# Sums of values over two halves of the keys, in 64x32 tiles, for two of eight groups of heads

## The chip, the cores and the metric

The kernel runs on one core of a Trainium2 chip. The metric is device time in microseconds (us), from the first to the last instruction of one execution with what lies around it; less is better. A core has five engines that run at once and wait for each other by semaphores: TensorE (PE: matmuls; PEld: its weight loads), VectorE (DVE), ScalarE (ACT), GpSimd (POOL) and SyncE (SP, which issues most DMAs). Matmuls write to PSUM, eight banks of 128 partitions x 512 fp32 values; ACT and DVE read them from there.

## What is computed

Two layers of self-attention, each followed by a dense block with squared ReLU, with the same weights both times. The sequence has 2048 rows of 640 values, 32 heads of 20 values each. Cut to what matters:

```
qkv = (x @ wqkv).reshape(B, S, 3, H, Dh).transpose(2, 0, 3, 1, 4)
q, k, v = qkv[0], qkv[1], qkv[2]
scores = einsum("bhqd,bhkd->bhqk", q, k) * (Dh ** -0.5)
p = softmax(scores, axis=-1)
o = einsum("bhqk,bhkd->bhqd", p, v)
A(x) = o.transpose(0, 2, 1, 3).reshape(B, S, D) @ wo
...
x = x + A(layernorm(x));  x = x + B(layernorm(x))
x = x + A(layernorm(x));  x = x + B(layernorm(x))
```

## The kernel before

Everything is written by hand in program order; nothing is scheduled by a planner. A layer has three stages: `qkv` (projections, and a part of the maxima), `attention`, and the output projection with the dense block.

The 32 heads are taken in 8 groups of 4 (g = 0 to 7), the queries in 4 blocks of 512. A block of a group (t = 4 g + query block, 32 in a layer) goes through 16 key tiles of 128 keys; one key tile of one block is called a step here, so a layer has 512 steps. For each step `attention` issues:

- four scores (`score`, L560), one for each head: 128 keys x 512 queries into one of PSUM banks 0 to 3. Operands are fp32r. Of the four heads, two lie in partitions 0 to 61 ("a" in the order, `par` 0) and two in 64 to 125 ("b", `par` 1), so a score takes a 64x128 tile of the array, half of its rows, and two scores of different halves can run side by side. ACT takes the exponential (L567) into an SBUF tile `e`, in fp32;
- sums of values (`pv`, L572; "V" in the order): for each of the four heads one fp32 matmul of the values (128 keys x 32, a column of ones among them, which gives the softmax's denominator) with the exponentials (128 keys x 512 queries). A matmul of 128 rows and 32 columns takes a 128x32 tile, and the four heads lie side by side in the columns. All 16 steps of a block accumulate in bank 7. Each fp32 matmul is issued as two;
- about three maxima (`smax`, L463 and L475; "m" for `par` 0, "n" for `par` 1): softmax needs the largest score of each query beforehand. TensorE computes 128 queries x 512 keys in a 64x128 tile into one of banks 4, 5 and 6, taken in turn (`sm_ring`), and DVE reduces it to one column of `mx`. These belong to blocks some steps ahead; when a block's maxima are complete, they are turned into two more rows of the operand `q`.

The order within PE's program comes from written-out strings. `pairs()` chooses by how many maxima are still due how many of each kind (12 to 16) go into the next eight steps, and `ORDERS` has one string for each such number. At 12 it is:

```
12: "naambbmVanmbambVbmannabVnabnmabVabnmbanVbbmnanaVbmmbaanVbmbmnaaV",
```

Values of a step come one step after its scores: V of step i follows the scores of step i + 1. `state["begun"]` is the last step whose scores have begun, `state["done"]` the next one whose values are due. Within a half of the rows, or where a bank has to be free first, instructions wait in this order.

At the end of a block `finish` (L585) copies bank 7 to an SBUF tile `o` on DVE; POOL and DMAs then divide by the denominators. The whole PSUM is in use in this stage: banks 0 to 3 scores, 4 to 6 maxima, 7 values.

Of the kernel before, what the change touches and what calls it, by code (L numbers as in the profile page):

```python
# [16 lines left out]
P = 128  # L17
# [8 lines left out]
NQB = S // QB  # L26
NG = H // 4
NKT = S // P
# [11 lines left out]
def tile_layers(  # L40
# [11 lines left out]
    nc = tc.nc  # L52
# [10 lines left out]
    def name(p):  # L63
        n_alloc[0] += 1
        return f"{p}{n_alloc[0]}"

    def slot(shape, dtype, label):
        return arena.tile(shape, dtype, tag="slot", name=name(label))

    def dma(eng, dst, src):  # L70

        if dst.dtype == F32R:
            dst = dst.bitcast(F32)
        if src.dtype == F32R:
            src = src.bitcast(F32)
        eng.dma_start(dst, src)
# [4 lines left out]
    banks = psum.tile([P, 8, 512], F32, tag="banks", name="banks")  # L81
# [183 lines left out]
    def split_to(dst_hi, dst_lo, src):  # L265

        nc.scalar.copy(dst_hi, src)  # L267
        nc.vector.tensor_sub(dst_lo, src, dst_hi.bitcast(F32))  # L268
# [9 lines left out]
    def pool_hi(dst, src):  # L278
        nc.gpsimd.tensor_copy(dst, src)  # L279

    def pool_lo(dst, a, b):
        nc.gpsimd.tensor_sub(dst, a, b)  # L282
# [123 lines left out]
    k_t, q_t, v_t, mx_t, kept = {}, {}, {}, {}, {}  # L406
    left, done, split = {}, set(), {}
# [25 lines left out]
    def load_q(t):  # L433
        g, qb = divmod(t, NQB)
        q_t[t] = slot([P, 2, QB], F32R, "q")
        rows_of_heads(q_t[t], d_qk[0, :, :, qb * QB : (qb + 1) * QB], QSEG, g)
# [16 lines left out]
    def maxima(t):  # L453
        if t not in mx_t:
            mx_t[t] = small.tile([P, 4, 4, 4], F32, tag="mx", bufs=14, name=name("mx"))
            if t in PARTLY:
                nc.vector.memset(mx_t[t], LEAST)
        return mx_t[t]

    def by_queries(dst, t, p, sub, c, par):  # L460

        b = 64 * par
        nc.tensor.matmul(  # L463
            dst,
            q_t[t][b : b + 60, p, sub * P : (sub + 1) * P],
            k_t[t // NQB, c][b : b + 60, p, :],
            start=True,
            stop=True,
        )

    def smax(ring, t, p, sub, c, par):

        dst = ring("sm")
        by_queries(dst, t, p, sub, c, par)
        nc.vector.tensor_reduce(  # L475
            maxima(t)[:, 2 * p + par, sub, c : c + 1], dst, axis=AX.X, op=ALU.max
        )
# [73 lines left out]
    def score(t, kt, h, es):  # L551

        p, par = divmod(h, 2)
        if p not in es:
            es[p] = weights[len(e_n) % len(weights)]
            e_n.append(t)
        dst = ps_st("st")
        b = 64 * par
        assert t in done
        nc.tensor.matmul(  # L560
            dst,
            k_t[t // NQB, kt // 4][b : b + 62, p, (kt % 4) * P : (kt % 4 + 1) * P],
            q_t[t][b : b + 62, p, :],
            start=True,
            stop=True,
        )
        nc.scalar.activation(es[p][:, par, :], dst, AF.Exp, scale=SCALE)  # L567

    def pv(acc, t, kt, es, heads=(3, 2, 1, 0)):
        for h in heads:  # L570
            p, par = divmod(h, 2)
            nc.tensor.matmul(  # L572
                acc[32 * h : 32 * h + 32, :],
                v_t[t // NQB, kt // 8][:, kt % 8, 32 * h : 32 * h + 32],
                es[p][:, par, :],
                start=(kt == 0),
                stop=(kt == NKT - 1),
            )

    def finish(t, acc):  # L580


        g, qb = divmod(t, NQB)
        o = slot([P, 2, QB], F32, "o")
        nc.vector.tensor_copy(o[:, 0, :], acc)  # L585
        res = []

        def store(q):
            ot = res.pop().rearrange("p l t -> p (l t)")
            for h in range(4):  # L590
                r0 = (4 * g + h) * DH
                dma(q, d_o[r0 : r0 + DH, qb], ot[32 * h : 32 * h + DH])

        if t == NBLK - 1:

            def invert():
                dst = ps_all("rs")
                nc.tensor.matmul(dst, sums_t, o[:, 0, :], start=True, stop=True)
                nc.vector.reciprocal(o[:, 1, :], dst)

            def divide():
                nc.vector.tensor_mul(o[:, 0, :], o[:, 0, :], o[:, 1, :])
                res.append(slot([P, 2, QB], F32R, "ot"))
                split_to(res[0][:, 0, :], res[0][:, 1, :], o[:, 0, :])

            return [invert, divide, lambda: store(nc.scalar)]

        few = small.tile([P, 16], F32, tag="few", bufs=2, name=name("few"))
        for h in range(4):
            dma(nc.sync, d_s[t, h : h + 1], o[32 * h + DH : 32 * h + DH + 1, 0, :])  # L610

        def load():
            dma(nc.sync, few, d_s[t].rearrange("h (q j) -> (h q) j", j=16))

        def invert():
            nc.gpsimd.tensor_tensor(few, few, minus_t, op=ALU.pow)  # L616

        def spread():
            dma(nc.sync, d_r[t].rearrange("h (q j) -> (h q) j", j=16), few)

        def gather():
            for h in range(4):
                dma(nc.sync, o[32 * h : 32 * h + 32, 1, :], d_r[t, h].partition_broadcast(32))

        def divide():
            ot = slot([P, 2, QB], F32R, "ot")
            nc.gpsimd.tensor_mul(o[:, 0, :], o[:, 0, :], o[:, 1, :])  # L627
            pool_hi(ot[:, 0, :], o[:, 0, :])
            pool_lo(ot[:, 1, :], o[:, 0, :], ot[:, 0, :].bitcast(F32))
            res.append(ot)  # L630

        return [load, invert, spread, gather, divide, lambda: store(nc.sync)]
# [230 lines left out]
    def attention(first, x_src, first_rows):  # L863
# [3 lines left out]
        weights.extend(slot([P, 2, QB], F32, "e") for _ in range(6))  # L867
        st_n, sm_n = [0, 0], [0, 0]
        state = {"begun": -1, "done": 0, "acc": None, "debt": 0}
        sm_ring = Ring(4, 5, 6)  # L870
        todo = [
            (t, p, sub, c)
            for t in range(NBLK)
# [15 lines left out]
        rows = {"next": min(t for t in range(NBLK) if t not in done), "at": None}  # L889
# [33 lines left out]
        def op(o):  # L923
            if o in "ab":
                par = "ab".index(o)
                i, p = divmod(st_n[par], 2)
                if i >= last:
                    return
                st_n[par] += 1
                if i > state["begun"]:  # L930
                    state["begun"] = i
                    begin(i)
                score(i // NKT, i % NKT, 2 * p + par, es_of.setdefault(i, {}))
            elif o in "mn":
                par = "mn".index(o)
                n = sm_n[par]
                if n == len(todo):
                    return
                t, p, sub, c = todo[n]
                if n == firsts[t] and par == 0:  # L940
                    for s in blocks[blocks.index(t) :][:2]:
                        if s not in q_t:
                            load_q(s)
                if (t // NQB, c) not in k_t or t not in q_t:
                    return
                sm_n[par] += 1
                smax(sm_ring, t, p, sub, c, par)
                if n == ends[t] and min(sm_n) > n:
                    over.add(t)
                    if t * NKT > state["begun"] + 2 * NKT:  # L950
                        del q_t[t]
            else:
                i = state["done"]
                if i >= last or min(st_n) < 2 * (i + 1):
                    return
                t, u = divmod(i, NKT)
                if u == 0:
                    state["acc"] = banks[:, 7, :]
                pv(state["acc"], t, u, es_of.pop(i))
                state["done"] += 1  # L960
                if u == NKT - 1:
                    steps = finish(t, state["acc"])
                    split.update((i + j, f) for j, f in zip((4, 6, 7, 9, 11, 12), steps))
                t = rows["next"]
                if rows["at"] is not None:
                    if state["begun"] >= rows["at"]:
                        mrows_load(t)
                        rows.update(next=t + 1, at=None)
                elif t in over and t in q_t and state["begun"] >= (t - 2) * NKT + 4:
                    mrows_max(t)  # L970
                    mrows(t)
                    rows["at"] = state["begun"] + 2
# [13 lines left out]
        for o in "abab":  # L986
            op(o)
# [109 lines left out]
    def layer(first, x_a, x_m, x_e, front_0, ahead):  # L1097
        qkv(first, x_a, front_0)
        xs = []
        attention(first, x_a, xs)  # L1100
        steps = []
        for i in sorted(split):
# [120 lines left out]
```

## Time and profile before

| | us |
|---|---|
| median of the runs shown | 3796.79 |
| lowest and highest of the runs | 3794.22, 3799.36 |
| the profiled execution's own time | 3801.53 |
| its span, from the first to the last instruction | 3799.7 |
| PE busy in the span | 3705.0 (98%) |
| DVE busy | 2807.6 (74%) |
| ACT busy | 2556.0 (67%) |
| POOL busy | 831.0 (22%) |

The profile is of one execution. An instruction's row names the line of the kernel, the engine, the operation, the tiles that it writes and reads ("out<-in"), for matmuls rows*columns of the weights, the count, the time, and after a bar or in brackets how long the engine stood idle before it and what released it. Matmuls overlap, and their ends are modelled, so the start of the next one says more than the length of one. A timeline's rows give start and length in us from the span's start; instructions of one kind that follow closely are merged into one row with their count. The attention stages lie at about 366 to 1450 us and 2257 to 3342 us.

### The profile page before, as it was taken

The numbers are of one execution on the slowest core, as the hardware profiler recorded it, in microseconds if no ns is written. First come the engines' busy times: TensorE is split into PE (matmuls) and PEld (weight loads), VectorE is DVE, ScalarE is ACT, GpSimd is POOL, SyncE is SP. The second block draws the span as 40 slices with busy tenths as digits, with TensorE's granted clock in tenths as the row PEclk, the third lists the DMA queues.
The fourth block names the chain that finished last, engine by engine and source line by source line (L and its number), as shares of the span: only waits on it lengthen the run. The fifth ranks groups of instructions, "written<-read, shape, count | busy, mean of one in ns | idle before, by whom it ended". The sixth has DMA issues, their size and how long they took to land.

```text
span 3799.7 us, 64213 instructions
## 1 busy us (share of the span) xinstructions
PE 3705.0 (98%) x23572; PEld 2130.6 (56%) x23572; DVE 2807.6 (74%) x4796; ACT 2556.0 (67%) x4887; POOL 831.0 (22%) x921
## 2 busy tenths in 40 slices
PE   7999999999999999799999999999999999998999
PEld 5677343443444338688876764434444444387888
DVE  7788999999999973344467889999999999633443
ACT  2555999999999993112224459999999999921221
POOL 6530333321221110111154201122121211101110
PEclk9999999999999999899999999999999999998999
DMA  7564454432211136311255533222222111463111
GB/s 220 191 209 143 135 143 151 140 83 80 59 45 45 43 114 233 135 42 42 93 185 170 176 125 82 74 75 60 65 78 63 43 45 43 124 228 127 42 45 40
DMA packets 256530, 402.27 MB, mean 106 GB/s; under 512 B 67580, under 2 KB 114428, under 8 KB 256216
## 3 DMA queue, kind: packets, MB, share of 16 engines
q1 hardware_dynamic: 255672, 396.45, 33.6%
q8 instruction: 187, 3.06, 0.3%
q10 hardware_dynamic: 544, 1.71, 0.2%
q14 instruction: 127, 1.04, 0.1%
HBM read 261.22 MB, written 136.81 MB: 105 GB/s over the span
## 4 chain that ended last, share of the span: by engine, by line
PE 91%; DVE 4%; DMA 2%; ACT 1%; POOL 1%; issue 0%; SPq 0%; ACTq 0%; POOLq 0%; DVEq 0%
PE banks L572 27%; PE banks L560 20%; PE banks L297 18%; PE banks L463 15%; PE banks L308 6%; PE banks L355 4%; DVE h L268 1%; DVE mx L484 1%; DVE bst L255 1%; DMA w<-d_w 1%; DVE r L1070 1%; ACT h L267 1%; PE banks L385 0%; PE banks L1043 0%; DMA x<-d_x 0%
## 5 line engine op out<-in xcount | busy, mean ns | idle before, releaser
L567 ACT ACTIVATE e<-banks 128x512 f32<-128x512 f32 x4096 | 2114.4, 604 | 62.0 <-PE banks L560 3.5
L475 DVE TENSOR_REDUCE mx<-banks 128x1 f32<-128x512 f32 x2940 | 1847.1, 684 | 186.3 <-PE banks L463 114.0
L463 PE MATMUL banks<-k,q 60*128 60x512 f32 x3744 | 1156.0, 437 | 9.0 <-DMA q<-d_qk 7.3
L560 PE MATMUL banks<-q,k 62*128 62x512 f32 x4096 | 1152.2, 435 | 2.1 <-DVE mx L484 1.7
L572 PE MATMUL banks<-e,vg 128*32 128x512 f32 x8192 | 1092.1, 605 | 0.0
L560 PEld LDWEIGHTS banks<-q,k 62*128 62x128 f32 x4096 | 601.5, 185 | 697.4 <-ACT e L567 664.8
L463 PEld LDWEIGHTS banks<-k,q 60*128 60x128 f32 x3744 | 537.8, 185 | 335.6 <-DVE mx L475 206.3
L297 PE MATMUL banks<-w,h 128*128 128x320 f32 x2304 | 380.0, 323 | 51.6 <-ACT h L267 40.1
L297 PEld LDWEIGHTS banks<-w,h 128*128 128x128 f32 x2304 | 357.4, 197 | 66.1 <-ACT h L267 46.6
L572 PEld LDWEIGHTS banks<-e,vg 128*32 128x32 f32 x8192 | 161.7, 108 | 357.4 <-issue 330.3
L495 ACT ACTIVATE rl<-banks 128x512 f32<-128x512 f32 x352 | 191.3, 596 | 247.3 <-PE banks L463 247.1
L297 PE MATMUL banks<-xnT,w 128*128 128x512 f32 x1440 | 330.7, 390 | 0.0
L308 PE MATMUL banks<-xnT,wqk 128*128 128x512 f32 x1200 | 319.9, 410 | 1.3 <-POOL wqk L282 1.3
L1069 ACT ACTIVATE r<-banks,b_t 128x512 f32<-128x512 f32 x96 | 66.0, 688 | 370.8 <-PE banks L297 370.8
L505 DVE CUSTOM_DVE_ANT_0 rl<-banks,rl 128x512 f32<-128x512 f32 x352 | 229.2, 689 | 111.4 <-PE banks L463 101.6
L297 PEld LDWEIGHTS banks<-xnT,w 128*128 128x128 f32 x1440 | 270.2, 188 | 55.3
L484 DVE TENSOR_REDUCE mx<-banks 128x2 f32<-128x1024 f32 x226 | 271.7, 1220 | 20.0 <-PE banks L463 19.2
L308 PEld LDWEIGHTS banks<-xnT,wqk 128*128 128x128 f32 x1200 | 217.8, 191 | 85.9 <-issue 43.9
L616 POOL TENSOR_TENSOR few<-few,minus_t 128x16 f32<-128x16 f32 x62 | 179.8, 2900 | 285.7 <-DMA few<-d_s 285.7
L1089 DVE TENSOR_TENSOR x<-banks,x 128x320 f32<-128x320 f32 x128 | 62.8, 491 | 216.5 <-PE banks L297 216.5
L627 POOL TENSOR_TENSOR o<-o 128x512 f32<-128x512 f32 x62 | 79.6, 1283 | 620.5 <-DMA o<-d_r 342.4
L279 POOL CAST mr<-nt 128x32 fp32r<-128x32 f32 x64 | 13.4, 209 | 804.1 <-DVE nt L531 804.1
(73 smaller groups left out, 2019.7 us busy)
## 6 DMA issues: line engine op xcount, KB each, us to landing
q<-d_qk SPq DMA_DIRECT2D x744, 80.0 KB
d_qk<-ev SPq DMA_DIRECT2D x80, 512.0 KB
k<-d_qk SPq DMA_DIRECT2D x468, 80.0 KB
x<-d_x SPq DMA_DIRECT2D x88, 320.0 KB
d_o<-ot SPq DMA_DIRECT2D x248, 80.0 KB
ot<-d_o SPq DMA_DIRECT2D x38, 512.0 KB
d_v<-v SPq DMA_DIRECT2D x32, 512.0 KB
vg<-d_v SPq DMA_DIRECT2D x32, 512.0 KB
```

Source lines behind the costliest of these rows:

```text
L297: nc.tensor.matmul(dst, a, b, start=(n == 0), stop=(n == last))
L308: nc.tensor.matmul(dst, w_qk.piece(pos * 10 + hw * KD + k), xt_[tb][k][:, hx, :], start=(n == 0), stop=(n == 3 * KD - 1),)
L355: nc.tensor.matmul(dst[:, :HALF], xt_[tb][k][:, hx, i * P : (i + 1) * P], w_v.piece(k * 4 + hw * 2 + hf), start=(j == 0), stop=(j == 3 * K ...
L463: nc.tensor.matmul(dst, q_t[t][b : b + 60, p, sub * P : (sub + 1) * P], k_t[t // NQB, c][b : b + 60, p, :], start=True, stop=True,)
L475: nc.vector.tensor_reduce(maxima(t)[:, 2 * p + par, sub, c : c + 1], dst, axis=AX.X, op=ALU.max)
L484: nc.vector.tensor_reduce(maxima(t)[:, 2 * p : 2 * p + 2, sub, c], dst, axis=AX.X, op=ALU.max)
L495: nc.scalar.activation(res[par], dst[:, par, :], AF.Relu)
L505: nc.vector.tensor_tensor_reduce(out=r[par], in0=dst[:, par, :], in1=r[par], scale=1.0, scalar=LEAST, op0=ALU.add, op1=ALU.max, accum_out= ...
L560: nc.tensor.matmul(dst, k_t[t // NQB, kt // 4][b : b + 62, p, (kt % 4) * P : (kt % 4 + 1) * P], q_t[t][b : b + 62, p, :], start=True, stop ...
L567: nc.scalar.activation(es[p][:, par, :], dst, AF.Exp, scale=SCALE)
L572: nc.tensor.matmul(acc[32 * h : 32 * h + 32, :], v_t[t // NQB, kt // 8][:, kt % 8, 32 * h : 32 * h + 32], es[p][:, par, :], start=(kt == 0 ...
L616: nc.gpsimd.tensor_tensor(few, few, minus_t, op=ALU.pow)
```

## The change

In two of the eight groups of heads (numbers 4 and 6, counted from 0) the value sums are taken over two halves of a key tile: keys 0 to 63 go into bank 7, keys 64 to 127 into bank 6. Each matmul has 64 rows and 32 columns (a 64x32 tile), and there are eight of them in a step instead of four, each issued as two. At the end of such a block DVE copies the first bank and adds the second. While a step of such a group is begun or due, maxima take turns in banks 4 and 5 only. The order strings are as before, and so are all other groups.

```
+    HALVES = (4, 6)
+
     def pv(acc, t, kt, es, heads=(3, 2, 1, 0)):
+        n = P // len(acc)
         for h in heads:
             p, par = divmod(h, 2)
-            nc.tensor.matmul(
-                acc[32 * h : 32 * h + 32, :],
-                v_t[t // NQB, kt // 8][:, kt % 8, 32 * h : 32 * h + 32],
-                es[p][:, par, :],
-                start=(kt == 0),
-                stop=(kt == NKT - 1),
-            )
+            for i, a in enumerate(acc):
+                rows = slice(i * n, (i + 1) * n)
+                nc.tensor.matmul(
+                    a[32 * h : 32 * h + 32, :],
+                    v_t[t // NQB, kt // 8][rows, kt % 8, 32 * h : 32 * h + 32],
+                    es[p][rows, par, :],
+                    start=(kt == 0),
+                    stop=(kt == NKT - 1),
+                )
...
-        nc.vector.tensor_copy(o[:, 0, :], acc)
+        nc.vector.tensor_copy(o[:, 0, :], acc[0])
+        for a in acc[1:]:
+            nc.vector.tensor_add(o[:, 0, :], a, o[:, 0, :])
...
-        sm_ring = Ring(4, 5, 6)
+        sm_ring, sm_two = Ring(4, 5, 6), Ring(4, 5)
...
-                smax(sm_ring, t, p, sub, c, par)
+                few = any(state[n] // (NKT * NQB) in HALVES for n in ("begun", "done"))
+                smax(sm_two if few else sm_ring, t, p, sub, c, par)
...
-                    state["acc"] = banks[:, 7, :]
+                    state["acc"] = [banks[:, 7, :]] + [banks[:, 6, :]] * (t // NQB in HALVES)
```

## The prediction

> **What bounds the kernel now.** I read the page first (shares, the chain that ended last, the costliest groups), then the busy time of one group of heads, then single instructions of one step.
>
> ```profile
> span 3799.7 us, 64213 instructions
> ...
> PE 91%; DVE 4%; DMA 2%; ACT 1%; POOL 1%; issue 0%; SPq 0%; ACTq 0%; POOLq 0%; DVEq 0%
> PE banks L572 27%; PE banks L560 20%; PE banks L297 18%; PE banks L463 15%; PE banks L308 6%; PE banks L355 4%; DVE h L268 1%; DVE mx L484 1%; DVE bst L255 1%; DMA w<-d_w 1%; DVE r L1070 1%; ACT h L267 1%; PE banks L385 0%; PE banks L1043 0%; DMA x<-d_x 0%
> ...
> L475 DVE TENSOR_REDUCE mx<-banks 128x1 f32<-128x512 f32 x2940 | 1847.1, 684 | 186.3 <-PE banks L463 114.0
> L572 PE MATMUL banks<-e,vg 128*32 128x512 f32 x8192 | 1092.1, 605 | 0.0
> L572 PEld LDWEIGHTS banks<-e,vg 128*32 128x32 f32 x8192 | 161.7, 108 | 357.4 <-issue 330.3
> ```
> The chain is TensorE for 91%, with sums of values (L572), scores (L560) and maxima (L463) ahead. 8192 value matmuls are 8 for each of 1024 steps (2 layers x 32 blocks x 16 key tiles): each of a step's four fp32 matmuls is issued as two. One of the eight groups of heads, by the busy time of its stretch and by its groups:
>
> ```profile
> 910.43:1046.46 136.03, 136.03 (x961) 54.68 (x960) 124.02 (x205) 132.22 (x258) 26.03 (x24) 1.00 0.25 68
> ```
> ```profile
> L475 DVE TENSOR_REDUCE mx<-banks 128x1 f32<-128x512 f32 x193 | 121.3, 684 | 11.6 <-PE banks L463 6.8 <-PE banks L560 4.6
> L463 PEld LDWEIGHTS banks<-k,q 60*128 60x128 f32 x192 | 30.4, 185 | 16.7 <-DVE mx L475 13.4
> L585 DVE COPY o<-banks 128x512 f32<-128x512 f32 x4 | 2.7, 680 | 0.0
> ```
> After the stretch's length stand PE, PEld, DVE, ACT and POOL busy. PE is busy all through, ACT 132.22 of 136.03 us, DVE 124.02. A group is 64 steps, so a step is 136.03 / 64 = 2.126 us; it holds 193 / 64 = 3.0 maxima. One whole step on PE, in order of time (start, duration):
>
> ```profile
> 2610.71 1.06 PE L572 MATMUL banks<-e,vg 128*32 128x512 f32 x8
> ...
> 2611.16 0.61 PE L572 MATMUL banks<-e,vg 128*32 128x512 f32 x4
> 2611.70 0.50 PE L560 MATMUL banks<-q,k 62*128 62x512 f32 x1
> 2611.71 0.50 PE L463 MATMUL banks<-k,q 60*128 60x512 f32 x1
> 2612.04 0.39 PE L560 MATMUL banks<-q,k 62*128 62x512 f32 x1
> 2612.04 0.39 PE L463 MATMUL banks<-k,q 60*128 60x512 f32 x1
> 2612.27 0.40 PE L560 MATMUL banks<-q,k 62*128 62x512 f32 x1
> 2612.27 0.40 PE L463 MATMUL banks<-k,q 60*128 60x512 f32 x1
> 2612.51 0.39 PE L560 MATMUL banks<-q,k 62*128 62x512 f32 x1
> 2612.84 1.07 PE L572 MATMUL banks<-e,vg 128*32 128x512 f32 x8
> ```
> Values start at 2610.71, their second issue at 2611.16 (0.45 later, four heads at once), the first score 0.99 after the first value matmul. Scores and maxima run in pairs, one in each half of the rows: 0.34 from the first pair to the second, then 0.23 and 0.24; 0.33 from the last to the next values. So a change of tile size costs about 0.1 of drain each way, and another 0.11 where the first weights are not loaded ahead (0.50 against 0.39 for the first matmul).
>
> What DVE and the weight loads do in that step:
>
> ```profile
> 2610.76 1.28 DVE L475 TENSOR_REDUCE mx<-banks 128x1 f32<-128x512 f32 x2
> ...
> 2612.27 1.29 DVE L475 TENSOR_REDUCE mx<-banks 128x1 f32<-128x512 f32 x2 [0.23 <-PE banks L463]
> ```
> ```profile
> 2612.09 0.18 PEld L463 LDWEIGHTS banks<-k,q 60*128 60x128 f32 x1
> 2612.10 0.18 PEld L560 LDWEIGHTS banks<-q,k 62*128 62x128 f32 x1
> ```
> Two reduces end at 2610.76 + 1.28 = 2612.04; the third maximum's weights load at 2612.09, 0.05 later: with three banks it waits for the last reduce of the step before. The score behind it loads 0.01 later, so a maximum that waits holds up what follows it in PE's order. The first maximum (2611.71 + 0.50) is done at 2612.21 and reduced from 2612.27, 0.06 later. Three banks are just enough: the wait hides behind the second pair.
>
> **The change, part by part.** Forecast of the sum: 256 steps (2 layers x 2 groups x 64) get longer.
>
> *Values in halves.* A step's 8 issues become 16; each has 64 rows instead of 128 but the same 512 columns, and each of 8 tiles (before: of 4) again gets two issues of 0.45. If eight tiles run at once, the array's time is unchanged. The trace has four column tiles at once and two row tiles at once, never both; unchanged is the near end, double (0.90 more) the far one. I take unchanged, since both halves of the claim are shown. Eight weight loads of mean 0.108 us lie within 0.16 (the row of a step is below), 0.007 apart, so four more tiles end 0.03 later: +0.03.
>
> ```profile
> 2612.84 0.16 PEld L572 LDWEIGHTS banks<-e,vg 128*32 128x32 f32 x8 [0.37 <-issue]
> ```
> *Drain.* Scores are in 64x128 tiles, values now in 64x32: only the columns change. No row here shows such a change. The nearest is the projection stage, where only the rows change (128 columns on both sides):
>
> ```profile
> 250.78 0.31 PE L355 MATMUL banks<-wv,xnT 128*128 128x320 f32 x1
> 251.02 0.79 PE L463 MATMUL banks<-k,q 60*128 60x512 f32 x4
> 251.65 0.40 PE L463 MATMUL banks<-kd,q 60*128 60x512 f32 x2
> 251.97 0.71 PE L355 MATMUL banks<-wv,xnT 128*128 128x320 f32 x3
> ```
> Last pair to projection: 251.97 - 251.65 = 0.32, the same as the 0.33 above. So a change of one dimension already costs the whole drain. By that I let it stay; the other end is none: 0.99 - 0.90 = 0.09, 0.50 - 0.39 = 0.11 and 0.33 - 0.23 = 0.10, 0.30 off each step. The Trainium skill, "TensorEngine Tiling (Array Packing)", Key Properties, says that a change of tiling mode drains TensorE, and 64x128 and 64x32 are two of its modes: by it the drain stays and the time is the forecast, not the second case. The trace agrees for changes that touch the rows; no run here shows one of columns alone.
>
> *Two banks for maxima.* The third maximum of a step now uses the bank of the first, in the same step. It may load only when the first is computed and reduced: 0.50 (done) + 0.06 + 0.68 (reduce) + 0.05 = 1.29 after the step's first score. Today 2612.09 is 0.39 after it. What follows in PE's order waits too, values included. The order list of 12 pairs (the one used at 3.0 maxima per step) has eight steps:
> - n a a m b b m, a n m b a m b, b m m b a a n: first maximum in the first pair, nothing behind the third in its rows or nothing that adds. Values 0.44 after the third (0.33, and 0.11 for weights not loaded ahead): 0.99 + 0.03 + 1.29 + 0.44 = 2.75.
> - b m a n n a b, n a b n m a b, b m b m n a a: one more matmul in turn behind it: 0.99 + 0.03 + 1.29 + 0.34 + 0.33 = 2.98.
> - a b n m b a n, b b m n a n a: the first maximum counts as done 0.23 later (second in its rows, or counted only after the score ahead of it, as the next row shows): 2.75 + 0.23 = 2.98.
>
> ```profile
> 2608.26 3.78 DVE L475 TENSOR_REDUCE mx<-banks 128x1 f32<-128x512 f32 x6 [0.27 <-PE banks L560]
> ```
> That reduce of a maximum was released by a score. Mean (3 x 2.75 + 5 x 2.98) / 8 = 2.89, which is 0.77 over 2.126. Other ends: no added wait (0), or the whole shift of the load from 0.39 to 1.29 (0.90). The second maximum waits for nothing new: the third reduce ends about 0.8 after values start. 256 x 0.77 = 197 us. The two-bank ring starts about two steps before the values reach such a group, four times: 8 x 0.74 = 6 us.
>
> *End of a block.* A tensor_add from the second bank follows the copy, 16 times. Its price is bounded by these rows:
>
> ```profile
> L505 DVE CUSTOM_DVE_ANT_0 rl<-banks,rl 128x512 f32<-128x512 f32 x352 | 229.2, 689 | 111.4 <-PE banks L463 101.6 <-issue 5.0 <-ACT wqk L171 1.8
> L1089 DVE TENSOR_TENSOR x<-banks,x 128x320 f32<-128x320 f32 x128 | 62.8, 491 | 216.5 <-PE banks L297 216.5
> L572 PEld LDWEIGHTS banks<-e,vg 128*32 128x32 f32 x8192 | 161.7, 108 | 357.4 <-issue 330.3 <-DVE o L585 21.5 <-ACT e L567 2.2
> ```
> I take 0.69 (512 columns; 0.49 for 320 is the lower end, 0.79 in proportion the upper). DVE does copy and add (0.68 + 0.69) ahead of the next step's first reduce, which could have begun 0.50 after values end: 0.87 later, and the third maximum with it. 16 x 0.87 = 14 us; nothing if it were covered.
>
> *At nothing.* DMAs, exps, their banks and all other groups are untouched. ACT has 4 exps a step in a longer step, so exps stay covered.
>
> Sum: 197 + 6 + 14 = 217 us on the profiled execution (3801.53 us, span 3799.7). That one is 4.7 over the median 3796.79; the median becomes 3796.8 + 217 = 4014, +5.7%.
>
> **The rivals.**
> 1. *The drain between 64x128 and 64x32 goes away.* For it: half of the rows keep their tile height. Against: the 0.32 above. Steps of 2.89 - 0.30 = 2.59: 256 x 0.464 = 119, with 4 and 14: 3934 (+3.6%).
> 2. *Eight value tiles do not run at once.* For: never shown together. Against: each dimension alone is. 0.90 x 256 = 230 more: 4244.
> 3. *Not slower: later values pass the waiting maximum.* If PE took the value matmuls, which wait for no reduce, while the third maximum waits, their 0.99 us would cover the 0.90 of extra wait. Place: the third maximum of each step. Then +0.03 x 256 and 14: about 3819 (+0.6%); with the drain gone too, down to what ACT (3.8 us a group) or DVE (12.0 us) leave idle, four groups long: 3797 - 4 x 12.0 + 14 = 3763 at best. It decides once the added wait is under (76 - 14) / 256 = 0.24 us a step. Against it: the weights at 2612.10 behind the wait that ended at 2612.09. The Trainium skill, "TensorE: Matmul & The Clock Gate", section on packing small matmuls, has matmuls start in strict order, which would rule it out; the row of 2608.26 agrees that they are counted in order.
>
> **How the numbers follow.** Forecast (drain stays, third maximum waits) 0.50; drain gone 0.30; values at half rate 0.08; not slower 0.12. The first two have their own spreads: 0.05 a step either way on the wait (13 us), the add covered or not (14), the steps at the groups' ends (6): 3980 to 4050 and 3900 to 3965. The range 3895 to 4055 holds both and leaves out 0.20. 2% (76 us), about what a measurement of this kernel can tell from no change, lies below both. Faster by over 2% would need 3721, under the 3763 above: 0.01. Within 2%: 0.11. Slower: 0.88.
>
> **What would show it.** Right: value matmuls 64*32 x4096 (256 x 16) beside 128*32 x6144; stretches of groups 4 and 6 (counted from 0) of each layer near 188 us (64 x 2.89 + 4 x 0.87) instead of 136, others at 136; in them the weights of the third maximum load 0.05 after the first reduce's end, idle time of PEld L463 behind DVE grown by over 100 us. Drain: 0.99 (stays) or near 0.90 (gone) from values to the first score. Half rate: second value issues 0.9 after the first. Wrong also: if the waits let the clock drop. Today it is 1.00 in attention, but this stretch, with PE 81% busy in one long gap, was granted 0.88:
>
> ```profile
> 1500.00:1600.00 100.00, 80.81 (x445) 73.28 (x445) 32.77 (x54) 11.46 (x19) 10.55 (x12) 0.88 0.44 166
> ```
> PE would be busy some 75% to 85% in the changed steps, in gaps under 1 us.

## The result, and the profile after

The median went from 3796.79 to 4017.52 us (4015.73 to 4019.30), two executions of each, a ratio of 1.0578 with a 95% interval of 1.0552 to 1.0603: slower, as forecast (4014). The profiled execution took 4019.30 us, its span is 4017.5, 217.8 more than before (3799.7). One of the ten executions of a run below, `whole_two_maxima`, took 4923 us at a mean granted clock of 0.654; it has no profile, counts in no ratio, and what took its clock is open.

The page of the kernel after: span, engines, and the chain that ended last, by engine and by line. L577 is the line of the value sums now (L572 before).

```profile
span 4017.5 us, 68332 instructions
...
PE 3797.5 (95%) x25620; PEld 2135.7 (53%) x25620; DVE 2842.7 (71%) x4812; ACT 2570.2 (64%) x4887; POOL 832.6 (21%) x921
...
PE 86%; DVE 9%; DMA 2%; ACT 1%; issue 1%; POOL 1%; SPq 0%; DVEq 0%; ACTq 0%; POOLq 0%
PE banks L577 26%; PE banks L297 17%; PE banks L560 17%; PE banks L463 16%; PE banks L308 6%; DVE mx L475 4%; PE banks L355 4%; DVE h L268 1%; DVE bst L255 1%; DVE mx L484 1%; DVE r L1078 1%; DMA w<-d_w 1%; ACT h L267 1%; DMA x<-d_x 0%; PE banks L385 0%
```
DVE has gone from 4% to 9% of the chain, by the reduces of maxima (L475), which were not among the lines before. DVE was busy for longer only by 35 us; it is waited for more. PE is no longer busy all through: it fell from 98% to 95% of a longer span.

Where the time came from: the busy time of group 4 of the first layer (64 steps; length, then PE, PEld, DVE, ACT, POOL).

```profile
911.64:1100.94 189.30, 158.50 (x1473) 55.88 (x1472) 132.29 (x209) 135.41 (x257) 25.96 (x24) 1.00 0.18 49
```
189.30 us instead of 136.03, and the same within 0.1 in the other three such stretches: 4 x 53.3 = 213 us. The groups ahead of them are 1.6 to 2.0 us longer (the two-bank ring begins early), 4 x 1.8 = 7. All other groups' stretches are as before within 0.5 us. The granted clock is 1.00 in both.

One step of that stretch (its order is n a a m b b m) on PE, from the maximum and scores after one sum of values to the next; then the first reduce on DVE and the third maximum's weights:

```profile
979.91 0.64 PE L577 MATMUL banks<-e,vg 64*32 64x512 f32 x8
980.48 0.50 PE L463 MATMUL banks<-k,q 60*128 60x512 f32 x1
980.48 0.73 PE L560 MATMUL banks<-q,k 62*128 62x512 f32 x3
981.05 0.40 PE L463 MATMUL banks<-k,q 60*128 60x512 f32 x1
981.05 0.39 PE L560 MATMUL banks<-q,k 62*128 62x512 f32 x1
981.76 0.49 PE L463 MATMUL banks<-k,q 60*128 60x512 f32 x1 [0.32 <-DVE mx L475]
982.18 1.09 PE L577 MATMUL banks<-e,vg 64*32 64x512 f32 x16
983.20 0.49 PE L560 MATMUL banks<-q,k 62*128 62x512 f32 x1
```
```profile
981.01 0.69 DVE L475 TENSOR_REDUCE mx<-banks 128x1 f32<-128x512 f32 x1 [0.99 <-PE banks L463]
```
```profile
981.76 0.18 PEld L463 LDWEIGHTS banks<-k,q 60*128 60x128 f32 x1 [0.75 <-DVE mx L475]
```
The step's first maximum starts at 980.48 and is reduced from 981.01 to 981.70; the third maximum's weights load at 981.76, 1.28 after the first score (1.29 in the forecast). PE waits for it with an idle array (0.32 us by the modelled ends), then the values start 0.42 after the third maximum. From values to the first score it is 983.20 - 982.18 = 1.02, the 0.99 + 0.03 of the forecast. The second issues of the values before started at 979.91, so the first at 979.46 (0.45 earlier); from there to these it is 2.72 us; the forecast had 2.75 for this kind of step.

The groups of instructions that changed, over the whole run and with all shapes kept apart; the first line is of the kernel before:

```profile
L463 PEld LDWEIGHTS banks<-k,q 60*128 60x128 f32 x3744 | 537.8, 185 | 335.6 <-DVE mx L475 206.3 <-issue 52.5 <-DVE mx L484 13.3
...
L577 PE MATMUL banks<-e,vg 128*32 128x512 f32 x6144 | 819.4, 605 | 0.0
L463 PEld LDWEIGHTS banks<-k,q 60*128 60x128 f32 x3744 | 541.7, 185 | 564.5 <-DVE mx L475 440.4 <-issue 51.8 <-DVE mx L484 10.5
L577 PE MATMUL banks<-e,vg 64*32 64x512 f32 x4096 | 278.8, 601 | 0.0
L592 DVE TENSOR_TENSOR o<-banks,o 128x512 f32<-128x512 f32 x16 | 11.1, 692 | 1.7
```
The 4096 halves keep PE busy for 278.8 us; before, a quarter of the value work was 1092.1 / 4 = 273.0. So eight tiles run at once, as fast as four of twice the height. What grew is the idle time of the maxima's weight loads behind reduces: 440.4 us against 206.3.

### The profile page after: what moved, and what is told of

Read it like the earlier page. It is cut to its first block, busy times and chain, and to the rows that moved or that the text cites. A ratio compares the mean times of both kernels' runs of the same rounds, so it can differ in the third digit from the quotient of the medians.

```text
span 4017.5 us, 68332 instructions
## 1 busy us (share of the span) xinstructions
PE 3797.5 (95%) x25620; PEld 2135.7 (53%) x25620; DVE 2842.7 (71%) x4812; ACT 2570.2 (64%) x4887; POOL 832.6 (21%) x921
## 4 chain that ended last, share of the span: by engine, by line
PE 86%; DVE 9%; DMA 2%; ACT 1%; issue 1%; POOL 1%; SPq 0%; DVEq 0%; ACTq 0%; POOLq 0%
PE banks L577 26%; PE banks L297 17%; PE banks L560 17%; PE banks L463 16%; PE banks L308 6%; DVE mx L475 4%; PE banks L355 4%; DVE h L268 1%; DVE bst L255 1%; DVE mx L484 1%; DVE r L1078 1%; DMA w<-d_w 1%; ACT h L267 1%; DMA x<-d_x 0%; PE banks L385 0%
## 5 line engine op out<-in xcount | busy, mean ns | idle before, releaser
L475 DVE TENSOR_REDUCE mx<-banks 128x1 f32<-128x512 f32 x2940 | 1869.4, 685 | 354.0 <-PE banks L463 245.8
L463 PE MATMUL banks<-k,q 60*128 60x512 f32 x3744 | 1213.5, 442 | 134.5 <-DVE mx L475 119.2
L560 PE MATMUL banks<-q,k 62*128 62x512 f32 x4096 | 1189.5, 436 | 2.1 <-DVE mx L484 1.7
L577 PE MATMUL banks<-e,vg 128*32 128x512 f32 (+1 forms) x10240 | 1098.2, 603 | 0.0
L560 PEld LDWEIGHTS banks<-q,k 62*128 62x128 f32 x4096 | 592.2, 185 | 696.8 <-ACT e L567 654.2
L463 PEld LDWEIGHTS banks<-k,q 60*128 60x128 f32 x3744 | 541.7, 185 | 564.5 <-DVE mx L475 440.4
L577 PEld LDWEIGHTS banks<-e,vg 128*32 128x32 f32 (+1 forms) x10240 | 167.6, 106 | 341.4 <-issue 321.4
```

The source lines that it names most:

```text
L463: nc.tensor.matmul(dst, q_t[t][b : b + 60, p, sub * P : (sub + 1) * P], k_t[t // NQB, c][b : b + 60, p, :], start=True, stop=True,)
L475: nc.vector.tensor_reduce(maxima(t)[:, 2 * p + par, sub, c : c + 1], dst, axis=AX.X, op=ALU.max)
L560: nc.tensor.matmul(dst, k_t[t // NQB, kt // 4][b : b + 62, p, (kt % 4) * P : (kt % 4 + 1) * P], q_t[t][b : b + 62, p, :], start=True, stop ...
L577: nc.tensor.matmul(a[32 * h : 32 * h + 32, :], v_t[t // NQB, kt // 8][rows, kt % 8, 32 * h : 32 * h + 32], es[p][rows, par, :], start=(kt ...
```

## The experiments

The theory: in the changed groups the third maximum of a step waits until the first is computed and reduced, since it needs the same bank, and all that follows in PE's order waits with it. The rival: the 64x32 form costs the time, by tiles that do not run at once or by drains. Ten kernels were run; "stretch" is the length of the 64 steps of group 4 in the first layer (136.0 before, 189.3 with the change).

| run | median, us | ratio to before, 95% | stretch, us |
|---|---|---|---|
| the change | 4017.5 | 1.0578 (1.0552 to 1.0603) | 189.3 |
| two_banks_only | 3999.4 | 1.0528 (1.0513 to 1.0544) | 184.1 |
| halves_scores_in_three | 3938.1 | 1.0372 (1.0354 to 1.0389) | 169.8 |
| whole_scores_in_three | 3923.2 | 1.0328 (1.0313 to 1.0344) | 166.9 |
| halves_no_add | 4007.8 | 1.0551 (1.0535 to 1.0567) | 185.8 |
| halves_one_bank | 4786.5 | 1.2598 (1.2573 to 1.2623) | 379.7 |
| halves_two_maxima | 3808.0 | 1.0018 (1.0009 to 1.0028) | 136.6 |
| whole_two_maxima | 3787.7 | 0.9971 (0.9961 to 0.9981) | 132.2 |
| wide_no_change_of_tile | 3921.4 | 1.0320 (1.0305 to 1.0335) | 165.8 |
| halves_short_reduce | 3950.6 | 1.0401 (1.0384 to 1.0419) | 172.7 |
| halves_order_third_last | 3974.1 | 1.0470 (1.0453 to 1.0487) | 177.9 |

### The two parts of the change apart

`two_banks_only`, the change without its halves:

```
-state["acc"] = [banks[:, 7, :]] + [banks[:, 6, :]] * (t // NQB in HALVES)
+state["acc"] = [banks[:, 7, :]]
```


> Whole value sums (128x32, bank 7) everywhere, but maxima of groups 4 and 6 in two banks as in the change; bank 6 idle there. Theory (the third maximum of a step waits for the reduce of the first): nearly all of the loss stays. 4017.5 less 256 x 0.03 (16 issues) less 16 x 0.87 (the added add) = 3996 us; the two stretches of 64 steps near 184 us. Rival (the 64x32 form itself costs the time, by its drain or by tiles that do not run at once): back to 3797 to 3810, stretches near 136.

Measured: 3999.4 us, 5.28% over before, stretch 184.05:

```profile
912.07:1096.12 184.05, 156.73 (x961) 54.45 (x961) 129.14 (x204) 134.78 (x256) 25.92 (x24) 1.00 0.19 50
```
With the very matmuls of before (961 on PE) and one bank left empty, 48.0 of the 53.3 us are there. The rival falls for all but the rest of 5.3 us.

`halves_scores_in_three` and its control `whole_scores_in_three` take the second bank from the scores instead; the control has whole sums:

```
+ps_st, ps_three = Ring(0, 1, 2, 3), Ring(0, 1, 2)
...
-sm_ring, sm_two = Ring(4, 5, 6), Ring(4, 5)
+sm_ring, sm_two = Ring(4, 5, 6), Ring(3, 4, 5)
...
+score(ps_three if few() else ps_st, ...)
```


> Halves in 64x32 as in the change, but the bank for the second sum is taken from the scores: in groups 4 and 6 scores take turns in three banks (0 to 2), maxima in three (3 to 5). Theory: the wait of the third maximum is gone; what is left is a wait of the third and fourth score for exps, which the control with whole sums has too, so this one is 8 us (0.03 a step) to 22 us (with the add) over that control, near 3945 us. Rival (the 64x32 form costs the time): some 200 us over the control.

> Control for the run with halves and three banks for scores: the same banks in groups 4 and 6 (scores 0 to 2, maxima 3 to 5), whole value sums. By hand: the fourth score of a step waits for the exp of the first, some 0.5 us a step, 264 steps: 3797 + 130 = 3930 us. Theory and rival say nothing different of this one alone; the difference to the run with halves decides.

Measured: 3938.1 and 3923.2, 14.9 us apart, where 8 to 22 was expected and the rival had some 200. The stretch with halves, then that of the control:

```profile
913.28:1083.06 169.78, 158.11 (x1475) 57.83 (x1473) 127.09 (x209) 132.28 (x258) 25.97 (x24) 1.00 0.20 55
912.37:1079.29 166.92, 156.41 (x962) 56.13 (x960) 124.17 (x204) 131.66 (x256) 26.01 (x24) 1.00 0.20 56
```
The control itself is 7 us under its estimate. Its PE rows show the other wait, of a score for an exponential:

```profile
952.54 0.73 PE L560 MATMUL banks<-q,k 62*128 62x512 f32 x3
953.12 0.40 PE L463 MATMUL banks<-k,q 60*128 60x512 f32 x1
953.75 0.49 PE L560 MATMUL banks<-q,k 62*128 62x512 f32 x1 [0.24 <-ACT e L567]
```
So here the halves cost 2.9 us a stretch, the add included, and the bank that they need costs 31 (from the scores) or 48 (from the maxima).

### The wait by its own terms

`halves_short_reduce` shortens the reduce that is waited for; it takes the maximum over half of the keys only:

```
-    maxima(t)[:, 2 * p + par, sub, c : c + 1], dst, axis=AX.X, op=ALU.max
+    maxima(t)[:, 2 * p + par, sub, c : c + 1], dst[:, :n], axis=AX.X, op=ALU.max
...
+    smax(..., QB // 2 if few else QB)
```


> The change with the reduces of the maxima of groups 4 and 6 over half of their columns (256 of 512; the maximum then is one over half of the keys). By the reduces of 512 (0.684) and 1024 columns (1.220) one of 256 takes 0.42, 0.27 less. Theory: the third maximum loads 0.27 earlier and each of 264 steps ends so much earlier: 4017.5 - 71 = 3946 us. Rival (it waits for something else of the first maximum, its matmul or the order): no change, 4017.

Measured: 3950.6 us. The reduce took 422 ns:

```profile
L475 DVE TENSOR_REDUCE mx<-banks 128x1 f32<-128x256 f32 x150 | 59.8, 422 | 65.2 <-PE banks L463 44.0 <-PE banks L560 19.7
```
and the stretch fell by 189.3 - 172.7 = 16.6 us, 0.26 a step, for a reduce that is 0.26 shorter. With the change itself DVE is busy for 132.29 of 189.30 us, so it has room; it is the reduce's latency that sets the step and not DVE's load. The next run says the same with as many reduces of the full length.

`halves_order_third_last` changes where the maxima stand:

```
+0: "naambbmVmbbnaanV" * 4,
...
+if n == 12 and state["done"] // (NKT * NQB) in HALVES:
+    n = 0
```


> The change with another order in groups 4 and 6: each step has its first maximum in the first pair and its third as the last matmul before the values (naambbm and mbbnaan in turn). Theory by the table of steps: all steps at 2.75 instead of a mean of 2.89, 4017.5 - 256 x 0.14 = 3982 us. Rival (the order plays no part, the added time is the same in every step): 4017.

Measured: 3974.1 us, 8 under the expectation. Every step inside a block takes 2.72 to 2.73 us, from the start of one step's value matmuls to the next, where the change has these, in the order of the string:

```
naambbm 2.73  anmbamb 2.77  bmannab 3.00  nabnmab 2.96
abnmban 2.97  bbmnana 2.99  bmmbaan 2.75  bmbmnaa 3.00
```
The forecast had 2.75 for the first, second and seventh, 2.98 for the others.

`halves_one_bank` doubles the wait (`Ring(4)` in place of `Ring(4, 5)`).

> The change with a single bank (4) for maxima in groups 4 and 6: the suspected wait twice per step. Theory: the second maximum loads 1.29 us after the step's first score, the third another 1.29 later; mean step 2.89 + 1.29 = 4.18, 264 steps: 3797 + 264 x 2.05 + 14 = 4353 us, a stretch of 64 steps near 271. Rival (the wait for the reduce is a small part, the rest is the form): at most some tens of us over the 4017 of the change.

Measured: 4786.5 us, far more than the theory's 4353. While the clock is full, a step is near the 4.18 that was expected: one step of the second layer, where each maximum waits for the one before it,

```profile
3303.53 1.09 PE L577 MATMUL banks<-e,vg 64*32 64x512 f32 x16
3304.55 0.50 PE L560 MATMUL banks<-q,k 62*128 62x512 f32 x1
3304.55 0.50 PE L463 MATMUL banks<-k,q 60*128 60x512 f32 x1
3305.87 0.49 PE L463 MATMUL banks<-k,q 60*128 60x512 f32 x1 [0.81 <-DVE mx L475]
3305.87 0.73 PE L560 MATMUL banks<-q,k 62*128 62x512 f32 x2
3307.14 0.49 PE L463 MATMUL banks<-k,q 60*128 60x512 f32 x1 [0.55 <-DVE mx L475]
3307.15 0.49 PE L560 MATMUL banks<-q,k 62*128 62x512 f32 x1
3307.57 0.66 PE L577 MATMUL banks<-e,vg 64*32 64x512 f32 x8
```
has maxima 1.32 and 1.27 apart and takes 4.04 us. Then the granted clock falls. The last columns are clock, DMA share and GB/s; the last two rows are the stretch of group 4 and most of that of group 5, which has three banks:

```profile
3296.60:3308.20 11.60, 7.44 (x60) 2.44 (x58) 6.66 (x10) 6.19 (x12) 0.00 (x0) 1.00 0.25 73
1040.00:1070.00 30.00, 24.97 (x123) 7.46 (x116) 10.95 (x16) 11.12 (x21) 3.15 (x3) 0.50 0.08 20
914.72:1294.44 379.72, 305.59 (x1473) 91.96 (x1473) 138.91 (x208) 139.90 (x255) 25.87 (x24) 0.53 0.09 25
1298.00:1428.00 130.00, 130.00 (x920) 52.09 (x923) 117.94 (x195) 126.09 (x245) 25.99 (x24) 1.00 0.19 52
```
At 0.50 a step inside a block takes 5.8 to 6.2 us. The clock falls where the changed groups begin and is full again in the group between them, so it goes with the waits. The waits of PE in the stretch of group 4, in total, their number, and the longest:

```profile
PE banks L463 <- DVE mx L475: 74.2, 119, 1.1
```
The expectation left the clock out. The wait is confirmed by the steps at full clock; the total says nothing more of it.

### Without the third maximum

`halves_two_maxima` and its control `whole_two_maxima` leave out the third maximum of each step in the changed groups. The counter starts again after each step's values, and `mx` is set to 0 beforehand in all groups:

```
+state["third"] += 1
+if few and state["third"] == 3:
+    maxima(t)
+else:
     smax(...)
```


> The change with the third maximum of each step of groups 4 and 6 left out (its matmul and its reduce; the shift of the softmax starts from 0 instead, which it can). Two maxima in two banks: theory has no wait left; PE 0.99 + 0.03 + 0.34 + 0.23 + 0.33 = 1.92 a step, at the edge of ACT, so about 1.95; stretches near 127, total near 3765 us, and 5 to 20 us over the control with whole sums and three banks. Rival (the 64x32 form costs the time): 200 us over that control.

> Control: whole sums and three banks, the third maximum of each step of groups 4 and 6 left out in the same way. By hand 1.89 a step on PE, held by ACT at 1.91 to 1.95; stretches near 125, total 3797 - 4 x 11 = 3753 us.

Measured: 3808.0 and 3787.7. Their difference, 20 us, is at the edge of what was expected (5 to 20), and the rival's 200 is not there. The stretch with halves, then that of the control:

```profile
915.04:1051.64 136.60, 135.63 (x1411) 54.63 (x1410) 89.94 (x149) 131.21 (x259) 26.07 (x24) 1.00 0.24 68
912.81:1045.01 132.20, 132.20 (x899) 53.49 (x897) 86.72 (x144) 130.18 (x258) 26.07 (x24) 1.00 0.26 70
```
The halves cost 4.4 us a stretch here, four times 17.6. Most of it lies where a block ends: by the starts of the value matmuls, steps there are longer than in the control by 0.7 us at each of three ends and 1.3 at the last, together some 3.4. At the last PE waits for the add:

```profile
1050.98 0.50 PE L463 MATMUL banks<-k,q 60*128 60x512 f32 x1 [0.97 <-DVE o L592]
```
Both totals missed: 43 and 35 us over the expectation. The stretch of the control is 132.20, not 125. A step there takes 132.2 / 64 = 2.07 on average, where the expectation had 1.89 for PE's order by hand and 1.91 to 1.95 with ACT; single steps take 1.94 to 2.17. Some of them have a score that waits for an exponential:

```profile
955.71 0.18 PEld L560 LDWEIGHTS banks<-q,k 62*128 62x128 f32 x1 [0.15 <-ACT e L567]
```
ACT is busy for 130.18 of the 132.20 us. That ACT and the four banks of the scores hold the step at 2.07 is likely, but no run tests it. The control is 136.0 - 132.2 = 3.8 us shorter than the stretch of before, just what ACT left idle there. That the two meet so closely is partly luck, since ACT's own busy time also fell by 2.0.

### The drain, and the add

`wide_no_change_of_tile` keeps all but the change of tile size:

```
+wide = len(acc) > 1 and h == 3
+cols = slice(0, P) if wide else slice(32 * h, 32 * h + 32)
+if len(acc) > 1 and not wide:
+    continue
 nc.tensor.matmul(
-    a[32 * h : 32 * h + 32, :],
-    v_t[t // NQB, kt // 8][rows, kt % 8, 32 * h : 32 * h + 32],
+    a[cols, :],
+    v_t[t // NQB, kt // 8][rows, kt % 8, cols],
```


> The change with value sums as one matmul per half, of all 128 value columns with one head's exponentials (64x128 tiles, as the scores have; the sums of the other three heads are left out). Two tiles of two issues take as long as eight, so only the change of tile size is gone. If the drain and the late weights come from the change of columns: 0.91 from values to the first score, first maximum done after 0.39, values 0.34 after the third maximum; mean step 2.57, 81 us under the change: 3937 us. If they come from something else (the sums' banks, a semaphore): 1.0 from values to the first score and 4000 to 4017.

Measured: 3921.4 us, 96 under the change (81 expected), stretch 165.8 against 189.3: 0.37 a step. Values to the next matmuls, with scores and values both in tiles of 64 rows and 128 columns:

```profile
954.75 1.02 PE L581 MATMUL banks<-e,vg 64*128 64x512 f32 x4
955.21 0.80 PE L463 MATMUL banks<-k,q 60*128 60x512 f32 x1
955.21 0.79 PE L560 MATMUL banks<-q,k 62*128 62x512 f32 x1
```
The next pair enters 0.46 after the values start, behind their second issue, where the change has 1.02. So a change of columns alone drains the array; the Trainium skill, "TensorEngine Tiling (Array Packing)", Key Properties, says that any change of tiling mode does, and here the trace agrees. The 0.37 us a step are for the way there and back, with the weights that load late and some 0.03 for the sixteen issues in it.

`halves_no_add` leaves out the add at the end of a block:

```
-for a in acc[1:]:
-    nc.vector.tensor_add(o[:, 0, :], a, o[:, 0, :])
```


> The change with the add at the end of a block left out (the second half of the sum is not used). Theory: the step after each of 16 blocks' ends is 0.87 us shorter, 4017.5 - 14 = 4004 us. Rival (the add is covered): no difference, 4017.

Measured: 4007.8 us, and this stretch:

```profile
914.68:1100.44 185.76, 158.26 (x1473) 55.97 (x1473) 129.16 (x204) 134.83 (x256) 25.99 (x24) 1.00 0.19 50
```
It is 185.76 instead of 189.30, 0.89 less for each of its four blocks, 14.2 us over the kernel. The medians are only 9.8 apart, and in the runs' ratios the two intervals (1.0535 to 1.0567, 1.0552 to 1.0603) overlap, so the stretch decides it; outside the changed groups the profiled execution of this run was some 4 us longer. DVE at the end of the first block, with the change:

```profile
956.46 0.69 DVE L590 COPY o<-banks 128x512 f32<-128x512 f32 x1 [0.69 <-PE banks L577]
957.26 0.69 DVE L592 TENSOR_TENSOR o<-banks,o 128x512 f32<-128x512 f32 x1
957.87 1.96 DVE L475 TENSOR_REDUCE mx<-banks 128x1 f32<-128x512 f32 x3
```
The next step's first reduce begins behind the add. That step took 3.74 us; without the add the same step took 2.95, and the same order takes 2.73 inside a block. So at three of the four block ends the add costs 0.8 us, and at the last of the group 1.2 (3.39 and 2.15).

No version that does the whole work beat the kernel before: the halves bring no time back, since the drain stays, and each bank that they could take is in use.

## Why the prediction was right

- *Values in halves, unchanged plus 0.03.* Right: 1.02 from values to the first score, sixteen issues within 1.09, 278.8 us for 4096 where a quarter of the old work had 273.0. The rival of half rate (4244) is excluded by that row.
- *Drain stays.* Right by the same 1.02, and by the run with wide tiles. What its end would bring was set somewhat low: 0.30 a step in the first rival, 0.37 measured, of which the 0.03 of sixteen issues is a part. The row it was taken from showed a change of rows only; that columns alone cost the same was not shown before and is now.
- *Two banks, 0.77 a step.* Right. The stretch without the add is 185.76 / 64 = 2.903 a step, 0.777 over 2.126. The two kinds of steps came out as 2.73 to 2.77 and 2.96 to 3.00 (2.75 and 2.98), in the places where the table put them. That the time is a wait and not load or form is shown by the empty bank, the shorter reduce and the other order. The empty bank gives the wait alone: 48.0 / 64 = 0.75, for which the forecast had 0.77 - 0.03 = 0.74.
- *Later values pass the waiting maximum* (the rival that was not slower). Excluded: the 0.32 of idle array behind DVE ahead of the values at 982.18. The strict order of starts that the prediction cites against this rival is not what the trace of before shows across the two halves of the rows. In a step of order b b m n a n a, the maximum starts together with the first score, ahead of the second, which stands before it in the program:

```profile
2607.46 0.50 PE L560 MATMUL banks<-q,k 62*128 62x512 f32 x1
2607.46 0.50 PE L463 MATMUL banks<-k,q 60*128 60x512 f32 x1
2607.79 0.40 PE L560 MATMUL banks<-q,k 62*128 62x512 f32 x2
```
So the measured 0.32 excludes the rival, and the rule does not. The rival's best case, 3763, also went by DVE's idle time (12.0 us a group), though ACT with its 3.8 would have been the tighter bound: 3797 - 4 x 3.8 + 14 = 3796.

- *End of a block, 14 us.* Right: 14.2 for the add alone, where the forecast had copy and add together. The copy adds a little more (2.95 against 2.73 in the step above), which stands in the next sum within the 0.777. The price of the add, 0.69, was 0.692.
- *Ring that begins early, 6 us.* 7.
- *The sum.* 0.777 x 256 = 199, with 14 and 7: 220, forecast 217; the spans differ by 217.8, so some 2 us fell elsewhere, where stretches scatter by that much. That the forecast meets the spans' difference to 1 us is to this extent luck.
- *The clock.* It stayed at 1.00. The run with one bank shows that the doubt was in place: with two such waits in each step the clock goes. The row that the doubt came from (1500 to 1600 us) has not one long gap, as the prediction says, but six of 1.1 to 9.9 us.

## What to carry to other kernels

Before taking a buffer out of a ring, write down the order in which it is used and count which use will wait for which: with one buffer fewer, the wait moves from the step before into the step itself, and its price is the whole latency (matmul, hand-over, reduce, hand-over), not the engine's load. An engine that is idle a third of the time can still set the pace like that. A new tile shape has to be judged by the shapes on both sides of it: with half the rows the values had the scores' height, but the drain stayed, because the columns still differed.

## What the runs showed of the hardware

- Eight fp32 matmuls in 64x32 tiles run at once and take as long as four in 128x32: the sixteen issues of a step span 1.09 us, the eight before 1.06.
- The clock fell in the run with one bank (0.53 in the stretch of group 4) although the longest wait of PE there was 1.1 us. The Trainium skill, "TensorE: Matmul & The Clock Gate", Why this matters for your kernels, puts the return to half the clock at idle gaps over about 3 us; here the clock fell without such a gap. The length of the longest gap does not tell the two kernels apart, since with the change it was 1.3 us, at a clock of 1.00. The idle share at full clock differs: 1.36 of 4.04 us in the step of one bank shown above, 30.80 of 189.30 with the change. Where between the two the limit lies, and whether it goes by the share, no run shows. At 0.50 the busy share does not tell it: 24.97 of 30 us, as high as with the change (158.50 of 189.30), because slower matmuls fill the time.
- A change of columns alone (64x128 to 64x32) drains TensorE like one of rows: in `halves_two_maxima` the values start 0.33 after the last maximum (914.70 to 915.03), where a change of rows alone took 0.32 in the kernel before (251.65 to 251.97).
